# Where the row maxima, the reciprocals and the output weights' splits stand in the order of one cycle: attention mixed with a Fourier layer on one core

## The chip, the cores and the metric

One core of one Trainium2 chip runs the whole program. The metric is the device time of one execution in microseconds (us), the median of several runs. Engine names: PE is TensorE (matmuls; PEld its weight loads), DVE is VectorE, ACT is ScalarE, POOL is GpSimd, SP is the engine whose queue issues nearly all transfers here.

## The reference

Two sublayers of the same input `x` (2048 rows of 640) are mixed by a gate for each row. One is attention with 32 heads of 20 columns, the other the real part of a Fourier transform over columns and rows, as matmuls with given matrices.

```python
def _A_ref(x, wqkv, wo):                      # H = 32, Dh = 20
    qkv = (x @ wqkv).reshape(B, S, 3, H, Dh).transpose(2, 0, 3, 1, 4)
    q, k, v = qkv[0], qkv[1], qkv[2]
    scores = jnp.einsum("bhqd,bhkd->bhqk", q, k) * (Dh ** -0.5)
    o = jnp.einsum("bhqk,bhkd->bhqd", softmax(scores, -1), v)
    return o.transpose(0, 2, 1, 3).reshape(B, S, D) @ wo

def _B_ref(x, dft_seq_re, dft_seq_im, dft_hid_re, dft_hid_im):
    a = jnp.einsum("bsd,ed->bse", x, dft_hid_re)
    b = jnp.einsum("bsd,ed->bse", x, dft_hid_im)
    return jnp.einsum("ts,bse->bte", dft_seq_re, a) - jnp.einsum("ts,bse->bte", dft_seq_im, b)

g = sigmoid((x * gate_w).sum(-1, keepdims=True))
out = g * _A_ref(x, wqkv, wo) + (1 - g) * _B_ref(x, ...)
```

## The kernel before

**Units and steps.** Attention is cut into 32 units (`NU`), each a pair of heads and half of the queries, and each unit into 32 steps of two matmuls, one for each head. Every unit is walked twice. In the *maximum* walk ("m") PE computes a score tile of 128 queries by 512 keys (line 197), and DVE takes the maximum of each row (line 199, tile `mx`). In the *exp* walk ("e") PE computes the scores again, transposed and with the maxima subtracted (line 951), and ACT takes the exponential (line 953). The m walk runs `LEAD` = 41 steps ahead of the e walk.

**From maxima to the exp walk.** When a unit's last maximum is written, `s_end` notes the unit in the list `ends`. `max_nm` reduces the 64 partial maxima of each row to 16 negated ones (DVE, line 215, tile `nm`). `max_chain` transposes them on PE into a PSUM bank (line 233), DVE splits the result in two parts (lines 115 and 116, tiles `m1`, `m2`), and SP writes these as rows into the query tile `qst` (lines 241 and 242), two steps later in the order.

**Values.** `av_step` multiplies exponentials with values: four matmuls, one for each pair of head and query block (line 558), added up in one PSUM bank. `unit_end` then copies the bank out (`o`, line 565) and sets up the normalisation by steps counted from there: the row sums are stored to DRAM (`store_l`) and loaded back in another layout (`load_l`, tile `lc`), inverted on DVE (`recip`, line 579), stored and loaded spread out (`store_r`, `load_r`, tile `rb`), multiplied in on POOL (`norm`, line 589) and stored (`store_o`).

**The Fourier side** is the filler, written as a generator whose pieces PE does between the scores: first the column transform (line 380), then the row transform in seven products of eight units (`dft_step`, line 637), then the output projection (line 744). In the row transform each group of eight fills, `s`, needs a weight tile: two raw loads (`raw`, `raw2`), combined on POOL (line 517), cast on ACT and split on POOL (`part`, lines 113 and 116). In the last product `dft_step` also loads five rows of the output weights (`in_wo`, line 645) into a `raw` tile and splits them on POOL; `r` counts the fills since that load. There are three `raw` tiles.

**What sets the order.** Nothing is scheduled by cost: each engine executes in the order in which the Python code emits. The loop over cycles reads a string of `ORDERS`: "e" and "m" are one matmul of a walk, "F" a share of filler, "B" the burst. There are three stages: cycles of four steps while the column transform fills, 112 cycles of six steps (`k == 1`) while the row transform fills, and cycles of four steps for the output. In the middle stage the string has twelve "m":

```python
    ("ememeFFFFmeFFemFeFmFemFeFeFmeFFmeFFFFmmemmB", (0, 0, 0, 1, 0, 1), (1, 1, 0, 1, 0, 0)),
```

`burst` runs pending read-outs and casts, then two `av_step`s (three in the middle stage). A unit of 32 steps against cycles of six gives three cases that repeat every 16 cycles: its last maximum is the fourth, the eighth or the twelfth of a cycle, seven times each. `at_step(i, fn)` keeps a function for the moment when the e walk begins step i. `bank()` hands out the score and transpose tiles from five PSUM banks in rotation; a sixth holds the values.

Of the kernel before, what the change touches and what calls it, by code (L numbers as in the profile page):

```python
# [24 lines left out]
ND = D // P  # L25
# [5 lines left out]
NU = 2 * NP  # L31
# [46 lines left out]
def mix_kernel(ctx: ExitStack, tc: tile.TileContext, xa, wqk, wb, cdft, wo, out):  # L78
# [56 lines left out]
    def raw_tile():  # L135
        return work.tile([P, 1024], F32, name="raw", bufs=3)
# [40 lines left out]
        p, u = VISITS[n]  # L177
        return third["q"] if p == 14 else qst[place(p)][:, u * (S // 2) : (u + 1) * (S // 2)]

    mx, nms, ends, early = {}, {}, [], []  # L180
    now, later = [-1], {}

    def at_step(i, fn):
        later.setdefault(i, []).append(fn)
# [16 lines left out]
    def s_end(i):  # L201
        n, s = divmod(i, 32)
        if n < NU and s == 31:
            if now[0] < 0:
                max_nm(n)
            else:
                if early:
                    max_nm(n)
                ends.append(n)
        if s == 1 and 0 < n <= NU and now[0] < 0:  # L210
            max_chain(n - 1)

    def max_nm(n):
        nms[n] = small.tile([P, 16], F32, name="nm", bufs=2)
        dve.tensor_reduce(nms[n], mx.pop(n).rearrange("p h q c -> p (h q) c"), axis=AX.X, op=ALU.max, negate=True)
# [9 lines left out]
    def new_y(z):  # L225
        yp[z] = ps_y.tile([P, 512], F32, name=f"yp{z}")
        return yp[z]


    def max_chain(n):  # L230
        q = q_unit(n)
        pt = bank()[:16, :P]
        pe.transpose(pt, nms.pop(n), ident)  # L233
        m1 = small.tile([16, P], R, name="m1")
        m2 = small.tile([16, P], R, name="m2")
        split(m1, m2, pt, dve, dve)

        def rows():
            for h in range(2):
                b = 64 * h + KROWS  # L240
                sp.dma_start(f32(q[b : b + 1, :]), f32(m1[8 * h : 8 * h + 8, :]))
                sp.dma_start(f32(q[b + 1 : b + 2, :]), f32(m2[8 * h : 8 * h + 8, :]))

        if now[0] < 0:
            rows()
        else:
            at_step(now[0] + 2, rows)
# [196 lines left out]
    order = [1, ND + 1, 2, ND + 2, 3, ND + 3, 4, ND + 4]  # L444
# [16 lines left out]
    for n, c in enumerate(order):  # L461
        for t in range(4):
            m = 4 * n + t
# [23 lines left out]
    def a_tile(n, s):  # L487
        at[n, s] = group(n, s // HT)[:, s % HT]
        return at[n, s]
# [72 lines left out]
    def unit_end(i, n):  # L562
        p, u = VISITS[n]
        o = pa.tile([P, 512], F32, name="o", bufs=2)
        act.activation(o, av["tile"], AF.Copy)
        if n == NU - 1:
            tail["o"] = o
            return
        rb = pa.tile([P, 512], F32, name="rb")
        lc = pa.tile([P, 16], F32, name="lc")  # L570

        def store_l():
            sp.dma_start(l_scr[n], o.rearrange("(j r) c -> j r c", j=4)[:, DH])

        def load_l():
            sp.dma_start(lc, l_scr[n].rearrange("j (a b) -> (j a) b", b=16))

        def recip():
            dve.reciprocal(lc, lc)

        def store_r():
            sp.dma_start(r_scr[n].rearrange("j (a b) -> (j a) b", b=16), lc)

        def load_r():
            for j in range(4):
                sp.dma_start(rb[32 * j : 32 * j + 32, :], r_scr[n, j : j + 1].to_broadcast([32, 512]))

        def norm():
            pool.tensor_tensor(o, o, rb, op=ALU.mult)

        def store_o():
            for qc in range(2):
                for h in range(2):
                    j = 2 * qc + h
                    t0 = u * (S // 2) + qc * 512
                    r = (2 * p + h) * DH
                    sp.dma_start(o_scr[r : r + DH, t0 : t0 + 512], o[32 * j : 32 * j + DH, :])

        steps = (6, 10, 16, 23, 27, 34, 45) if n < NU - 4 else (1, 4, 7, 8, 11, 14, 16)
        for k, fn in zip(steps, (store_l, load_l, recip, store_r, load_r, norm, store_o)):  # L600
            at_step(i + k, fn)

# [11 lines left out]
    def dft_step(g):  # L614
        n, t, s = g // NS // HT, g // NS % HT, g % NS
        if s == 0:
            new_y(0), new_y(1)
            outs[n, t] = []
        if s % 8 == 0 and g // 8 + 3 < 2 * UNITS:
            cfin.append(load_c(g // 8 + 3))  # L620
        if s % 8 == 2 and g // 8 + 2 < 2 * UNITS:
            cfin[0][0]()
        if s == 8:
            for _, th, hf in PRODUCTS[n][2]:
                tt = th * HT + t
                y = None
                if (tt, hf) in signs:
                    y = apool[0].tile([P, HE], F32, name="yt", bufs=4)
                    sp.dma_start(y, y_scr[tt, :, hf * HE : (hf + 1) * HE])
                outs[n, t].append(y)  # L630
        c = cparts[g // 8]
        cs = slice((s % 8) * P, (s % 8 + 1) * P)
        a = at[n % 2, s]
        for z, (cz, az) in enumerate(((0, 0), (0, 1), (1, 0))):
            for h in range(2):
                r = slice(64 * h, 64 * h + 64)
                pe.matmul(yp[h][:, :HE], c[r, cz, cs], a[r, az], start=s == 0 and z == 0, stop=s == NS - 1 and z == 2)  # L637
            if z < 2:
                yield
        w = g % (HT * NS) - 16  # L640
        if n + 1 == len(PRODUCTS) and w >= 0:
            d, r = divmod(w, 16)
            if r == 0 and d < ND:
                wos[d] = raw_tile()[:, :D]
                sp.dma_start(wos[d], wo[:, d])
            if r == 5 and d < ND:
                raw = wos.pop(d)
                for h in range(2):
                    wos[d, h] = a_tile(1, 2 * d + h)
                    split(wos[d, h][:, 0], wos[d, h][:, 1], raw[:, h * HE : (h + 1) * HE], pool, pool)  # L650
        if s == NS - 1:
            m = apool[1].tile([P, HE], F32, name="m", bufs=2)
            y0, y1 = yp[0][:, :HE], yp[1][:, :HE]

            def read():
                act.activation(m, y0, AF.Copy)
                dve.tensor_tensor(m, y1, m, op=ALU.add)

            extras.append((now[0], read))
            for out_, y in zip(PRODUCTS[n][2], outs.pop((n, t))):  # L660
                extras.append((now[0] + 3, functools.partial(finish_y, out_, t, m, y)))
        yield
# [196 lines left out]
    for k, tt in enumerate(ROWS):  # L859
        i = out_start + 8 * k  # L860
# [72 lines left out]
    def score(kind):  # L933
        x = heads[kind]
        heads[kind] += 1
        i, z = divmod(x, 2)
        h = z ^ first[kind][(i - (LEAD if kind == "m" else 0) - 1 - base) % len(first[kind])]
        if kind == "m":
            s_mm(i, h)()
            if z:  # L940
                s_end(i)
            return
        if z == 0 and i <= total:
            begin(i)
        if i < total:
            n, s = divmod(i, 32)
            kt, qc = divmod(s, 2)
            q, k = q_unit(n), k_stack(n)
            b = 64 * h
            pt = bank()  # L950
            pe.matmul(pt, k[b : b + KROWS + 2, kt * P : (kt + 1) * P],  # L951
                      q[b : b + KROWS + 2, qc * 512 : (qc + 1) * 512], start=True, stop=True)
            act.activation(pts[n, kt, qc][:, h], pt, AF.Exp, scale=float(DH) ** -0.5)  # L953
            if z:
                end(i)

    def burst(c):
        for n in ends:
            if n not in nms:
                max_nm(n)  # L960
        k, _, i = phase(c)
        steps = 6 if k == 1 else 4
        run_extras(steps - 2)
        if k == 1:
            run_casts()
        for kt in range(i // 2, (i + steps) // 2):
            if k == 1 and ends and kt == (i + steps) // 2 - 1:
                max_chain(ends.pop(0))
            av_step(now[0], kt // NS, kt % NS, kt % NS == 0 and kt > i // 2)
        while ends:  # L970
            max_chain(ends.pop(0))
        if c in (HID - NS - 1, HID - 1):
            next_pool()
# [4 lines left out]
    for c in range(len(goals)):  # L978
        k, base, i = phase(c)
        order, *heads_ = ORDERS[k]  # L980
        first = dict(zip("em", heads_))
        early[:] = [c] if k == 1 else []
        for x, kind in enumerate(order):
            if kind == "F":
                fill(c)
            elif kind == "B":
                burst(c)
            else:
                score(kind)
            if k == 1 and x == len(order) // 2:  # L990
                run_loads(c - HID)
# [114 lines left out]
```

## Time and profile before

| what | value |
| --- | --- |
| median of 3 runs | 1869.56 us (1869.52 to 1870.79) |
| the profiled execution's own time | 1869.01 us |
| its span, first to last instruction | 1867.2 us |
| PE busy | 1850.2 us, 99% of the span |
| DVE, ACT, POOL busy | 1380.7, 1355.6, 1003.8 us |
| mean granted PE clock | 0.999 |

The span is 1.8 us under the execution's own time. A busy share is a mean over all stages. The chain that ended last follows the program back from its last instruction to what released each step, and shows where an engine other than PE set the time. A row of a timeline gives the start in us, the length in us, engine, line, operation, output and inputs, and in square brackets how long the engine had stood idle before it and what ended that. Matmuls are pipelined, so their rows overlap.

### The profile page before, as it was taken

How to read it: one execution, taken by the hardware profiler on the slowest of the kernel's cores; microseconds unless marked ns; L12 is line 12 of the kernel's file. 1: busy time of each engine (PE TensorE's matmuls, PEld its weight loads, DVE VectorE, ACT ScalarE, POOL GpSimd, SP SyncE). 2: the span in 40 equal slices, each digit the busy share in tenths (PEclk: the TensorE clock that was granted, in tenths of full speed). 3: DMA queues.
4: the chain of work that ended last, by engine and by line, in shares of the span. 5: the costliest groups of instructions: out<-in, count | busy, mean ns of one | idle time of the engine just before them, and what ended most of it. 6: DMA issues, size and time to landing. Idle time of an engine off the chain costs nothing.

```text
span 1867.2 us, 44796 instructions
## 1 busy us (share of the span) xinstructions
PE 1850.2 (99%) x17606; PEld 1360.0 (73%) x17606; DVE 1380.7 (74%) x2309; ACT 1355.6 (73%) x2645; POOL 1003.8 (54%) x832
## 2 busy tenths in 40 slices
PE   9999999999999999999999999999999999999998
PEld 8988777677676777777777777777777777776666
DVE  3044458787887888888888888888888888888853
ACT  4222158787877888888788888788888877878885
POOL 4334532121146676344678688655668766745544
PEclk9999999999999999999999999999999999999999
DMA  7754341222134673536577586646475856532233
GB/s 234 166 142 155 135 127 54 82 61 72 50 112 126 219 220 120 156 117 193 188 198 238 151 258 193 180 137 183 129 231 187 244 173 183 187 91 54 82 98 109
DMA packets 178771, 281.61 MB, mean 151 GB/s; under 512 B 44811, under 2 KB 113547, under 8 KB 178559
## 3 DMA queue, kind: packets, MB, share of 16 engines
q1 hardware_dynamic: 177599, 276.77, 49.1%
q0 software_dynamic: 960, 1.97, 0.6%
q8 instruction: 138, 2.26, 0.5%
q14 instruction: 74, 0.61, 0.1%
HBM read 214.61 MB, written 63.52 MB: 149 GB/s over the span
## 4 chain that ended last, share of the span: by engine, by line
PE 93%; DMA 4%; DVE 1%; POOL 1%; SPq 0%; issue 0%; ACT 0%; POOLq 0%; ACTq 0%; DVEq 0%
PE ps L558 23%; PE yp L637 18%; PE ps L951 16%; PE ps L197 13%; PE yp L380 7%; PE ps L119 4%; PE ps L121 4%; PE ps L120 4%; PE yp L744 3%; DVE mx L199 1%; DMA kst<-qk_scr 1%; DMA lc<-l_scr 1%; DMA raw<-in_wo 1%; DMA raw<-in_cdft 0%; POOL part L116 0%; PE ps L233 0%
## 5 line engine op out<-in xcount | busy, mean ns | idle before, releaser
L199 DVE TENSOR_REDUCE mx<-ps 128x1 f32<-128x512 f32 x2048 | 1281.3, 684 | 318.6 <-PE ps L197 248.0
L953 ACT ACTIVATE p<-ps 128x512 f32<-128x512 f32 x2048 | 1054.3, 613 | 292.6 <-PE ps L197 167.4
L951 PE MATMUL ps<-qst,kst 62*128 62x512 f32 x1920 | 725.9, 406 | 0.1
L197 PE MATMUL ps<-kst,qst 60*128 60x512 f32 x1920 | 668.3, 411 | 1.6 <-DVE mx L199 1.6
L637 PE MATMUL yp<-x,part 64*128 64x320 f32 x5376 | 631.1, 306 | 0.0
L637 PEld LDWEIGHTS yp<-x,part 64*128 64x128 f32 x5376 | 603.5, 185 | 7.1 <-ACT raw L390 0.4
L558 PE MATMUL ps<-p,v 128*21 128x512 f32 (+1 forms) x4096 | 483.3, 596 | 0.0
L116 POOL TENSOR_TENSOR part<-raw,part 128x1024 fp32r<-128x1024 f32 (+1 forms) x128 | 287.3, 2244 | 331.2 <-ACT part L113 307.5
L951 PEld LDWEIGHTS ps<-qst,kst 62*128 62x128 f32 x1920 | 341.3, 185 | 156.4 <-DVE mx L199 86.4
L197 PEld LDWEIGHTS ps<-kst,qst 60*128 60x128 f32 x1920 | 320.0, 184 | 15.0 <-issue 4.2
L558 PEld LDWEIGHTS ps<-p,v 128*21 128x21 f32 (+1 forms) x4096 | 101.7, 100 | 236.5 <-issue 226.8
L380 PE MATMUL yp<-wb,x 64*128 64x320 f32 x1920 | 223.8, 307 | 0.0
L380 PEld LDWEIGHTS yp<-wb,x 64*128 64x128 f32 x1920 | 209.5, 186 | 6.3 <-ACT raw L390 0.3
L391 POOL TENSOR_TENSOR raw<-raw 128x320 f32<-128x320 f32 x64 | 55.6, 868 | 267.6 <-ACT raw L390 227.8
L517 POOL TENSOR_TENSOR raw<-raw,raw 128x1024 f32<-128x1024 f32 x77 | 187.5, 2435 | 0.4 <-DMA raw<-in_cdft 0.4
L113 ACT ACTIVATE part<-raw 128x1024 fp32r<-128x1024 f32 (+2 forms) x121 | 123.4, 1020 | 6.5 <-POOL raw L517 4.3
L744 PE MATMUL yp<-x,part 64*128 64x320 f32 x768 | 102.2, 308 | 0.0
L116 POOL TENSOR_TENSOR x<-araw,x 128x320 fp32r<-128x320 f32 x112 | 97.5, 877 | 1.3
L340 ACT ACTIVATE p<-ps 128x512 f32<-128x512 f32 x40 | 23.7, 597 | 101.1 <-PE ps L121 98.1
L744 PEld LDWEIGHTS yp<-x,part 64*128 64x128 f32 x768 | 91.8, 186 | 1.0
L119 PE MATMUL ps<-x,part 128*128 128x512 f32 x200 | 79.9, 400 | 2.8 <-ACT x L113 2.6
L120 PE MATMUL ps<-x,part 128*128 128x512 f32 x200 | 78.3, 392 | 0.2 <-DVE x L116 0.2
(101 smaller groups left out, 1355.8 us busy)
## 6 DMA issues: line engine op xcount, KB each, us to landing
raw<-in_cdft SPq DMA_DIRECT2D x192, 512.0 KB
araw<-a_scr SPq DMA_DIRECT2D x192, 160.0 KB
qk_scr<-p SPq DMA_DIRECT2D x40, 512.0 KB
kst<-qk_scr SPq DMA_DIRECT2D x84, 160.0 KB
qst<-qk_scr SPq DMA_DIRECT2D x84, 160.0 KB
yt<-y_scr SPq DMA_DIRECT2D x80, 160.0 KB
a_scr<-raw SPq DMA_DIRECT2D x64, 160.0 KB
y_scr<-yt SPq DMA_DIRECT2D x64, 160.0 KB
```

The lines of the kernel that those rows point to most:

```text
L116: e2.tensor_tensor(dst2, src, f32(dst1), op=ALU.subtract)
L119: pe.matmul(ps, st1, mv1, start=first, stop=False)
L120: pe.matmul(ps, st1, mv2, start=False, stop=False)
L197: pe.matmul(ps, q[b : b + KROWS, qt * P : (qt + 1) * P], k[b : b + KROWS, kc * 512 : (kc + 1) * 512], start=True, stop=True)
L199: return lambda: dve.tensor_reduce(mx[n][:, h, qt, kc : kc + 1], ps, axis=AX.X, op=ALU.max)
L380: pe.matmul(yp[h][:, :HE], x[r, xz, d, cs], w[r, wz, d, :HE], start=d == 0 and z == 0, stop=d == ND - 1 and z == 2)
L517: pool.tensor_tensor(raws[0], raws[0], raws[1], op=ALU.add if PRODUCTS[n][0][1][0] > 0 else ALU.subtract)
L558: pe.matmul(t[32 * j : 32 * j + m, :], v[:, r : r + m], pp[qc][:, h, :], start=kt == 0, stop=kt == NS - 1)
L637: pe.matmul(yp[h][:, :HE], c[r, cz, cs], a[r, az], start=s == 0 and z == 0, stop=s == NS - 1 and z == 2)
L744: pe.matmul(yp[h][:, :HE], o[oz][r], wos[d, hf][r, wz], start=d == 0 and z == 0, stop=end)
L951: pe.matmul(pt, k[b : b + KROWS + 2, kt * P : (kt + 1) * P], q[b : b + KROWS + 2, qc * 512 : (qc + 1) * 512], start=True, stop=True)
L953: act.activation(pts[n, kt, qc][:, h], pt, AF.Exp, scale=float(DH) ** -0.5)
```

## The change

Four places are edited. In the middle stage `nm` is no longer reduced directly behind a unit's last maximum: it is reduced ahead of the cycle's ninth maximum, if the unit has ended by then, and in the burst if it ends with the cycle (twelfth maximum). Only in the first case does the transpose stand ahead of the burst's last `av_step`; in the other it now comes behind it. In `unit_end` the reciprocal, its store and load and the normalisation move by 4, 2, 2 and 3 steps, for all but the last four units. The output weights are split at the eleventh fill behind their load instead of the fifth.

```diff
-    mx, nms, ends, early = {}, {}, [], []
+    mx, nms, ends = {}, {}, []
...
             else:
-                if early:
-                    max_nm(n)
                 ends.append(n)
...
-        steps = (6, 10, 16, 23, 27, 34, 45) if n < NU - 4 else (1, 4, 7, 8, 11, 14, 16)
+        steps = (6, 10, 20, 25, 29, 37, 45) if n < NU - 4 else (1, 4, 7, 8, 11, 14, 16)
         for k, fn in zip(steps, (store_l, load_l, recip, store_r, load_r, norm, store_o)):
...
-            if r == 5 and d < ND:
+            if r == 11 and d < ND:
                 raw = wos.pop(d)
...
     def burst(c):
+        ready = any(n in nms for n in ends)
         for n in ends:
             if n not in nms:
                 max_nm(n)
...
-            if k == 1 and ends and kt == (i + steps) // 2 - 1:
+            if ready and kt == (i + steps) // 2 - 1:
                 max_chain(ends.pop(0))
             av_step(now[0], kt // NS, kt % NS, kt % NS == 0 and kt > i // 2)
...
-        early[:] = [c] if k == 1 else []
...
             else:
+                if k == 1 and kind == "m" and order[:x].count("m") == 8:
+                    for n in ends:
+                        max_nm(n)
                 score(kind)
```

In the changed kernel the lines from `s_end` to the burst have numbers lower by two, and those behind the last edit higher by one.

PE's order at the burst of the first unit that ends with a cycle's twelfth maximum (`ps_9539` is that score, `ps_9560` the transpose), before:

```order
L197 MATMUL ps_9539<-kst_86,qst_88 128x512
L558 MATMUL ps_9059<-p,v 21x512 x8
L233 MATMUL ps_9560<-ident,nm 16x128
L558 MATMUL ps_9059<-p,v 21x512 x4
L951 MATMUL ps_9571<-qst_88,kst_86 128x512
L197 MATMUL ps_9575<-kst_87,qst_89 128x512
L951 MATMUL ps_9578<-qst_88,kst_86 128x512
L197 MATMUL ps_9581<-kst_87,qst_89 128x512
L951 MATMUL ps_9589<-qst_88,kst_86 128x512
```

The same place in the changed kernel:

```order
L197 MATMUL ps_9538<-kst_86,qst_88 128x512
L556 MATMUL ps_9058<-p,v 21x512 x12
L231 MATMUL ps_9563<-ident,nm 16x128
L949 MATMUL ps_9570<-qst_88,kst_86 128x512
L197 MATMUL ps_9574<-kst_87,qst_89 128x512
L949 MATMUL ps_9577<-qst_88,kst_86 128x512
L197 MATMUL ps_9580<-kst_87,qst_89 128x512
L949 MATMUL ps_9589<-qst_88,kst_86 128x512
```

The transpose has moved behind the last four `av_step` matmuls, directly ahead of the next cycle's scores; five tiles later its bank is used again, by the third exp score.

DVE's order around the same burst, with the reciprocal of an earlier unit, before:

```order
L579 RECIPROCAL lc<-lc 128x16
L199 TENSOR_REDUCE mx<-ps_9474 128x1
L199 TENSOR_REDUCE mx<-ps_9498 128x1
L199 TENSOR_REDUCE mx<-ps_9508 128x1
L199 TENSOR_REDUCE mx<-ps_9527 128x1
L199 TENSOR_REDUCE mx<-ps_9530 128x1
L199 TENSOR_REDUCE mx<-ps_9536 128x1
L199 TENSOR_REDUCE mx<-ps_9539 128x1
L215 TENSOR_REDUCE nm<-mx 128x16
L115 CAST m_9562<-ps_9560 16x128
L116 TENSOR_TENSOR m_9563<-ps_9560,m_9562 16x128
L199 TENSOR_REDUCE mx<-ps_9575 128x1
```

and in the changed kernel:

```order
L199 TENSOR_REDUCE mx<-ps_9535 128x1
L199 TENSOR_REDUCE mx<-ps_9538 128x1
L213 TENSOR_REDUCE nm<-mx 128x16
L115 CAST m_9565<-ps_9563 16x128
L116 TENSOR_TENSOR m_9566<-ps_9563,m_9565 16x128
L199 TENSOR_REDUCE mx<-ps_9574 128x1
L199 TENSOR_REDUCE mx<-ps_9580 128x1
L577 RECIPROCAL lc<-lc 128x16
L199 TENSOR_REDUCE mx<-ps_9606 128x1
```

On DVE the order around `nm` is as it was; the reciprocal has moved from behind the fifth maximum of a cycle to behind the second of the next.

POOL's order around the third of the five output weight splits (`x_24245` and `x_24362` are the tile written, the rows with two `raw` the combining additions), before:

```order
L517 TENSOR_TENSOR raw<-raw,raw_24644 128x1024
L115 CAST x_24245<-raw 128x320
L116 TENSOR_TENSOR x_24245<-raw,x_24245 128x320
L115 CAST x_24245<-raw 128x320
L116 TENSOR_TENSOR x_24245<-raw,x_24245 128x320
L771 TENSOR_TENSOR yt<-yt,m 128x320
L116 TENSOR_TENSOR part<-raw,part 128x1024
L517 TENSOR_TENSOR raw<-raw,raw_24811 128x1024
```

and in the changed kernel:

```order
L515 TENSOR_TENSOR raw<-raw,raw_24640 128x1024
L769 TENSOR_TENSOR yt<-yt,m 128x320
L116 TENSOR_TENSOR part<-raw,part 128x1024
L515 TENSOR_TENSOR raw<-raw,raw_24811 128x1024
L115 CAST x_24362<-raw 128x320
L116 TENSOR_TENSOR x_24362<-raw,x_24362 128x320
L115 CAST x_24362<-raw 128x320
L116 TENSOR_TENSOR x_24362<-raw,x_24362 128x320
L116 TENSOR_TENSOR part<-raw,part 128x1024
```

The split has moved behind the next combining addition, one weight tile later.

## The prediction

> **What bounds the kernel now.** I read the page first (its parts 1, 4 and 5), then the chain that ended last in order of time, then the timelines of DVE, PE, POOL and ACT at the places the chain points to.
>
> ```profile
> PE 1850.2 (99%) x17606; PEld 1360.0 (73%) x17606; DVE 1380.7 (74%) x2309; ACT 1355.6 (73%) x2645; POOL 1003.8 (54%) x832
> PE 93%; DMA 4%; DVE 1%; POOL 1%; SPq 0%; issue 0%; ACT 0%; POOLq 0%; ACTq 0%; DVEq 0%
> L951 PEld LDWEIGHTS ps<-qst,kst 62*128 62x128 f32 x1920 | 341.3, 185 | 156.4 <-DVE mx L199 86.4
> ```
>
> PE is busy for 1850.2 of 1867.2 us and carries 93% of the chain, so the end moves only where PE's work is held up. The change alters no arithmetic; it can win only the few per cent of the chain on DMA, DVE and POOL. The last row says that a weight load of the exp scores (L951) is itself what waits when a PSUM bank is still being read by DVE.
>
> The kernel repeats a cycle that ends in a burst of `av_step` matmuls (L558). In the chain the bursts are therefore a clock, and the distance of two starts is a cycle's length. Picked rows:
>
> ```profile
> 332.32 1.85 PE ps L558 x16
> 338.48 1.85 PE ps L558 x16
> 344.86 1.85 PE ps L558 x16
> ...
> 674.09 2.70 PE ps L558 x24
> 683.07 2.50 DVE mx L199 x4
> 693.74 2.70 PE ps L558 x24
> ...
> 721.67 2.71 PE ps L558 x24
> 731.08 2.70 PE ps L558 x24
> 740.62 1.84 PE ps L558 x16
> ...
> 778.26 2.70 PE ps L558 x24
> ...
> 1042.62 1.84 PE ps L558 x16
> ...
> 1070.53 7.42 DMA lc<-l_scr
> 1080.90 2.70 PE ps L558 x24
> ...
> 1147.39 2.70 PE ps L558 x24
> ...
> 1175.08 8.44 DMA lc<-l_scr
> 1186.54 2.70 PE ps L558 x24
> ...
> 1403.68 2.70 PE ps L558 x24
> ...
> 1451.24 2.70 PE ps L558 x24
> ...
> 1554.71 2.70 PE ps L558 x24
> ...
> 1593.86 2.50 DVE mx L199 x4
> 1604.51 2.70 PE ps L558 x24
> ```
>
> An undisturbed cycle of six steps: 693.74 to 721.67 is three cycles, 9.31 us each. A pattern of three units takes 16 cycles, about 151 us, and comes seven times in the product stage. What lies above 9.31 is what the change can reach.
>
> **The change part by part.**
>
> *1. Transpose behind the burst (seven units).* Where a unit's last maximum is the twelfth of its cycle, DVE still owes four maxima when the burst begins: the chain leaves PE for "DVE mx L199 x4" at 683.07, and so seven times, the last at 1593.86. From 674.09 to 693.74 are 19.65 us: one cycle with a reciprocal (9.41, below) and one with this transpose, 10.24, that is 0.93 over 9.31.
>
> ```profile
> 685.86 0.28 PE L233 MATMUL ps<-ident,nm 128*16 128x128 f32 x1 [0.53 <-DVE nm L215]
> ...
> 340.27 0.28 PE L233 MATMUL ps<-ident,nm 128*16 128x128 f32 x1
> 340.47 0.50 PE L951 MATMUL ps<-qst,kst 62*128 62x512 f32 x1
> 340.90 0.28 DVE L116 TENSOR_TENSOR m<-ps,m 16x128 fp32r<-16x128 f32 x1
> ...
> 667.42 0.50 PE L951 MATMUL ps<-qst,kst 62*128 62x512 f32 x1
> 668.00 0.98 PE L637 MATMUL yp<-x,part 64*128 64x320 f32 x9
> ```
>
> Of the 0.93, PE stands 0.53 at the transpose (685.86). The third `av_step` (a third of 2.70, 0.90) now runs in that gap and more than fills it. The transpose itself stays on the path. Behind a burst it stands already in the first stage: the cycle from 338.48 takes 6.38, the one before 6.16, so 0.22. One thing is new. The banks rotate by five, so the transpose's bank is wanted again by the fifth tile, the third exp score of the next cycle. In the first stage filler stands ahead of that score; here the order begins "ememe" and the score comes at once: five scores take 0.58 (667.42 to 668.00), the first begins 0.20 behind the transpose (340.27 to 340.47), so the third exp score would begin 0.78 after it. DVE has read the bank only at 341.18, 0.91 after. PE then waits 0.13, or 0.13 plus a load of 185 ns = 0.32. I take 0.25, nearer the upper, since the loads are seen waiting themselves. New excess 0.47, gain 0.46, times seven: 3.2 us. Ends: 5.0 without a bank wait (0.93 - 0.22), 1.6 with twice the price (0.93 - 0.22 - 0.48 = 0.23).
>
> The Trainium skill says (TensorE: Matmul & The Clock Gate, the section on the array's architectural detail) that PE's queue can pull weight loads ahead of running matmuls. By that rule the wait would be 0.13 alone and the sum 0.8 us better; the row of L951's loads, idle 156.4 us and mostly until DVE was done, speaks against it at a bank that is not free.
>
> Behind the transpose DVE's two small operations come later against the burst, but the maxima that they hold up are late too. The four row DMAs wait on them in SP's queue, about 0.3 later; their unit starts some ten steps on, so no cost.
>
> *2. Negated maximum ahead of the ninth maximum (seven units).* Where the unit ends with the fourth maximum, `nm` stands in a dense run.
>
> ```profile
> 736.36 0.69 DVE L199 TENSOR_REDUCE mx<-ps 128x1 f32<-128x512 f32 x1 [0.17 <-PE ps L197]
> 737.08 0.22 DVE L215 TENSOR_REDUCE nm<-mx 128x16 f32<-128x64 f32 x1
> 740.20 2.49 DVE L199 TENSOR_REDUCE mx<-ps 128x1 f32<-128x512 f32 x4 [0.42 <-PE ps L197]
> ```
>
> The run behind it is 0.2 late, banks come free late, and the cycle takes 9.54 (731.08 to 740.62): 0.23. Its new place is the pause of 0.42 ahead of the ninth maximum (740.20), longer than its 0.22. Gain 0.23 x 7 = 1.6; ends 1.0 and 1.7. Where the unit ends with the eighth maximum nothing moves.
>
> *3. Reciprocals four steps on (21 in the product stage).*
>
> ```profile
> 680.58 0.24 DVE L579 RECIPROCAL lc<-lc 128x16 f32<-128x16 f32 x1
> 680.74 1.93 DVE L199 TENSOR_REDUCE mx<-ps 128x1 f32<-128x512 f32 x3
> ```
>
> A reciprocal pushes the next maximum by 0.16 and costs a cycle 0.10 (721.67 to 731.08 is 9.41). Its new place is behind the second maximum of a cycle, where a pause of 0.17 follows one maximum later (736.36). It just fits: 0.09 x 21 = 1.9 gained; ends 0 (as dear there) and 2.1. Two of them wait for their transfer. 1042.62 to 1080.90 is 38.28, the same four cycles from 740.62 to 778.26 are 37.64: 0.64 more, with the load of `lc` landing 7.42 after its issue. 1147.39 to 1186.54 is 39.15 for four cycles, 693.74 to 731.08 is 37.34: 1.81 more, landing after 8.44. Four steps are two thirds of 9.31, 6.2 us, more than three times either wait, so 2.4 us go; ends 0.6 and 2.5.
>
> The Trainium skill puts a transfer at about 2.0 us plus its bytes over 436 GB/s (DMA: Bandwidth & Descriptors, Anatomy of one DMA), 2.02 us for these 8 KB as an estimate. By that no reciprocal would wait and this term would be nothing; here the rows measure 7.42 and 8.44.
>
> What follows a reciprocal moves too. Its store goes from step 23 to 25, five steps behind instead of seven; SP already stands waiting for the reciprocal in some units, and behind that store it stands at the row DMAs anyway, so nothing is held up. The four `rb` loads keep four steps to the store. The normalisation moves three steps on POOL and is the second rival's subject. Seven reciprocals of the first stage land in the same slot of the next cycle, at no cost.
>
> *4. Output weight splits six fills on (five, last product).*
>
> ```profile
> 1578.96 0.45 POOL L115 CAST x<-raw 128x320 fp32r<-128x320 f32 x1 [7.61 <-DMA raw<-in_wo]
> ...
> 1587.26 1.06 ACT L113 ACTIVATE part<-raw 128x1024 fp32r<-128x1024 f32 x1 [3.60 <-POOL raw L517]
> ```
>
> POOL waits 7.61 for a weight row; the combining addition behind it (L517) is late; ACT's cast waits 3.60 for that, and the exponentials queue behind the cast. 1554.71 to 1604.51 is 49.80; the same five cycles from 1403.68 to 1451.24 are 47.56. The difference is 2.24. Six fills of eight are three quarters of a cycle, about 7 us; the load itself no longer waits for a late POOL, so the wait is nearly gone: 2.2; ends 0 and 2.3. A split then holds its raw tile longer, until about five fills before the next weight load wants one: covered.
>
> **Sum.** 3.2 + 1.6 + 1.9 + 2.4 + 2.2 = 11.3 us. The profiled execution took 1869.01, so 1857.7; the runs' median is 1869.56, 0.55 above it, and the prediction is for that: 1858.3. All good ends give 13.6 (1856.0).
>
> **The rivals.** *Given back on DVE and in the banks.* The transpose wins only 1.6 and the reciprocals nothing. For it: both new places have a margin of hundredths. Then 1.6 + 1.6 + 2.4 + 2.2 = 7.8, 1861.8.
>
> *Slower: POOL falls behind.* The normalisation now comes ahead of a combining addition instead of behind one.
>
> ```profile
> 654.02 1.28 POOL L589 TENSOR_TENSOR o<-o,rb 128x512 f32<-128x512 f32 x1
> 660.44 2.43 POOL L517 TENSOR_TENSOR raw<-raw,raw 128x1024 f32<-128x1024 f32 x1
> 665.09 1.05 ACT L113 ACTIVATE part<-raw 128x1024 fp32r<-128x1024 f32 x1
> ```
>
> The addition ends at 662.87, ACT's cast begins at 665.09: 2.22 of slack, 0.94 after the 1.28 of the normalisation. Where POOL runs more than that behind, the exponentials wait. The price is near 2.0 per 3.60 of ACT's wait (part 4); to pass the 11.3 and another 3.7 it must strike with full force in eight of 21 units, 16.0 us, which ends at 1874.3. POOL is busy 54%, so unlikely.
>
> *Transfers stay late.* The waits of parts 3 and 4 meet another waiter: 3.2 + 1.6 + 1.9 = 6.7, 1862.9. Against it: both transfers landed well inside the time that is added.
>
> *No transfer ever bound.* The late reciprocals cost nothing by themselves, and PE was late for another reason at both places; without those 2.4 us, 1860.7. This is what follows if transfers take the skill's 2.02 us (the page on DMA above); the chain contradicts it twice.
>
> That the change does nothing is excluded: the orders of PE, DVE and POOL differ at just these places.
>
> **How the numbers follow.** The forecast 0.65 (its own range 1856.0 to 1861.0); given back 0.12; late transfers 0.10; no transfer bound 0.04; slower through POOL 0.04; smaller gains than any of these, within 0.2%, 0.05. A difference under 0.2%, 3.7 us, can't be told from none. Faster 0.65 + 0.12 + 0.10 + 0.04 = 0.91, same 0.05, slower 0.04. The range goes from 1 us under the good ends, 1855.0, past the late transfers with half a microsecond, 1863.5.
>
> **What the next profile would show.** Right: the seven chains through "DVE mx L199 x4" gone; PE's idle time at L233 near 0; cycles with that transpose about 9.8; none of 9.4 or 9.54; no `lc` load and no `in_wo` in the chain; ACT's wait for L517 gone. Wrong: exp scores (L951) idle at DVE's L116 behind a burst by more than 0.5; cycles still at 9.4 with the reciprocal early in them; longer waits of ACT's cast for L517; POOL waiting long for `in_wo` still.

## The result, and the profile after

The changed kernel takes 1856.76 us, median of four runs (1855.66 to 1858.53), against 1869.54 for the kernel before on the same chip (1868.96 to 1870.79): ratio 0.9932, 95% interval 0.9914 to 0.9949. Forecast were 1858.3 and a range of 1855.0 to 1863.5. The profiled execution of the changed kernel, the longest of the four, took 1858.53.

From the page of the changed kernel, PE's busy time, the chain's shares by engine, and the weight loads of the exp scores:

```profile
PE 1847.3 (99%) x17606; PEld 1362.8 (73%) x17606; DVE 1380.5 (74%) x2309; ACT 1356.0 (73%) x2645; POOL 1002.9 (54%) x832
PE 99%; DMA 0%; DVE 0%; ACT 0%; POOL 0%; SPq 0%; POOLq 0%; issue 0%; ACTq 0%
L949 PEld LDWEIGHTS ps<-qst,kst 62*128 62x128 f32 x1920 | 341.6, 185 | 154.3 <-DVE mx L199 86.4
```

The same work is on every engine, but PE now carries 99% of the chain instead of 93%. The shares of DMA, DVE and POOL, which were all that the change could reach, are gone.

The chain after, bursts (start, length, engine, line), the stretches that were shown of before:

```profile
684.20 2.70 PE ps L556 x24
693.99 2.71 PE ps L556 x24
...
731.21 2.70 PE ps L556 x24
750.17 2.70 PE ps L556 x24
...
1068.82 2.70 PE ps L556 x24
1078.11 2.70 PE ps L556 x24
...
1171.95 2.70 PE ps L556 x24
1181.23 2.71 PE ps L556 x24
...
1547.04 2.70 PE ps L556 x24
1594.33 2.70 PE ps L556 x24
```

The cycle with the late transpose is 9.79 (684.20 to 693.99; it was 10.24). 731.21 to 750.17 is 18.96 for the cycle in which `nm` stood early and the one behind it; it was 9.54 + 9.62. The two cycles whose reciprocal waited for `lc` are 9.29 and 9.28. The five cycles with the output weights are 47.29, before 49.80. From here on a cycle has a number, counted from the program's first value burst, the distance of two such starts taken from the full list of instructions; the product stage is cycles 56 to 166, and was 11.3 us shorter.

Timelines of DVE and PEld around that late transpose, and of DVE where a unit ends with the fourth maximum:

```profile
686.32 0.22 DVE L213 TENSOR_REDUCE nm<-mx 128x16 f32<-128x64 f32 x1
687.46 0.28 DVE L116 TENSOR_TENSOR m<-ps,m 16x128 fp32r<-16x128 f32 x1
687.79 0.18 PEld L949 LDWEIGHTS ps<-qst,kst 62*128 62x128 f32 x1 [0.45 <-DVE m L116]
688.87 0.23 DVE L577 RECIPROCAL lc<-lc 128x16 f32<-128x16 f32 x1
689.97 0.69 DVE L199 TENSOR_REDUCE mx<-ps 128x1 f32<-128x512 f32 x1 [0.17 <-PE ps L197]
...
739.70 0.21 DVE L213 TENSOR_REDUCE nm<-mx 128x16 f32<-128x64 f32 x1
740.09 2.48 DVE L199 TENSOR_REDUCE mx<-ps 128x1 f32<-128x512 f32 x4 [0.18 <-PE ps L197]
```

In the third row the load of the third exp score stands idle for 0.45 until DVE has read the transpose's bank at 687.74: this is the bank wait that the forecast added to the price of the move. The reciprocal and the other `nm` fit in their pauses, with 0.17 and 0.18 to spare.

### The profile page after: what moved, and what is told of

It reads as the page before. It is cut to its first block, busy times and chain, and to the rows that moved or that the text cites. A ratio compares the mean times of both kernels' runs of the same rounds, so it can differ in the third digit from the quotient of the medians.

```text
span 1856.7 us, 44810 instructions
## 1 busy us (share of the span) xinstructions
PE 1847.3 (99%) x17606; PEld 1362.8 (73%) x17606; DVE 1380.5 (74%) x2309; ACT 1356.0 (73%) x2645; POOL 1002.9 (54%) x832
## 4 chain that ended last, share of the span: by engine, by line
PE 99%; DMA 0%; DVE 0%; ACT 0%; POOL 0%; SPq 0%; POOLq 0%; issue 0%; ACTq 0%
PE ps L556 25%; PE yp L635 19%; PE ps L949 17%; PE ps L197 15%; PE yp L378 7%; PE ps L119 4%; PE ps L120 4%; PE ps L121 4%; PE yp L742 3%; DMA p<-in_xa 0%; PE ps L231 0%; DVE mx L199 0%; PE ps L1041 0%; POOL x L1010 0%; PE yp L1062 0%; POOLq L1103 0%
## 5 line engine op out<-in xcount | busy, mean ns | idle before, releaser
L951 ACT ACTIVATE p<-ps 128x512 f32<-128x512 f32 x2048 | 1054.9, 613 | 284.8 <-PE ps L197 177.2
```

## The experiments

**Four parts, one at a time.** The theory: the terms are independent, and each is worth what the sum says. The rivals give the gain of one part to another. Each ran once: 1865.44 us with the transpose alone, 1868.42 with `nm`, 1862.99 with the steps, 1867.27 with the weight splits, 1870.75 for the kernel before beside them. Transfers that are late in one execution and not in the next are in these times, so the parts are read from cycle lengths.

*The transpose alone.*

```diff
+        ready = any(n in nms for n in ends)
...
-            if k == 1 and ends and kt == (i + steps) // 2 - 1:
+            if ready and kt == (i + steps) // 2 - 1:
...
-        early[:] = [c] if k == 1 else []
+                early[:] = [c] if k == 1 and order[:x].count("m") < 11 else []
```

> The kernel before with the first edit alone: the transpose of a unit that ends with a cycle's twelfth maximum stands behind the burst; nm stays directly behind the last maximum, reciprocals and weight splits stay. My theory: the seven cycles with that transpose go from 10.24 to 9.78 us, every other cycle keeps its length (9.54 where nm follows the fourth maximum, 9.40 with a reciprocal), and the product stage is 7 x 0.46 = 3.2 us shorter. Rival: the 9.78 of the changed kernel holds a reciprocal that now falls in the same cycle and costs it 0.09 there; then these cycles take 9.69 here, 3.9 us in all. Second rival: the gain needs the moved nm or reciprocal; then they stay above 10.0.

```profile
685.25 2.70 PE ps L558 x24
695.05 2.70 PE ps L558 x24
```

9.80 here; over the seven 9.78 to 9.81, together 3.1 us. The reciprocal that the changed kernel has in the same cycle is therefore free.

*`nm` alone.*

```diff
-                if early:
-                    max_nm(n)
...
+                if k == 1 and kind == "m" and order[:x].count("m") == 8:
+                    for n in ends:
+                        max_nm(n)
                 score(kind)
```

> The kernel before with the second edit alone: nm is reduced ahead of the cycle's ninth maximum, the transpose always stands ahead of the burst's last av_step. My theory: the seven cycles whose unit ends with the fourth maximum go from 9.54 to 9.31 us, 7 x 0.23 = 1.6 us, the cycles with the late transpose stay 10.24, all others as before. Rival (the pause of 0.42 doesn't take it in, and the reciprocals' move made the room in the changed kernel): they keep 9.40 or more, at most 1.0 us in all.

```profile
730.90 2.70 PE ps L556 x24
749.84 2.70 PE ps L556 x24
...
1068.97 8.40 DMA lc<-l_scr
```

18.94 for the two cycles; the seven went from 9.54 to 9.30, 1.7 us. The last row is the load of `lc` that ends at 1077.37, in the cycle that waited 0.6 in the trace of before: here 0.9. The whole product stage was only 0.5 us shorter: the wait of cycle 116 was gone (1.8), but another, for the output weights in cycle 159, took 2.4 more than in the trace of before, and three others 0.8 more together.

*The steps alone.*

```diff
-        steps = (6, 10, 16, 23, 27, 34, 45) if n < NU - 4 else ...
+        steps = (6, 10, 20, 25, 29, 37, 45) if n < NU - 4 else ...
```

> The kernel before with the seven steps of the normalisation alone moved. My theory: the cycles with a reciprocal go from 9.40 to 9.31 us, the two that waited for lc from 9.98 and 11.24 to 9.3, cycle 159 (its reciprocal 8.5 us behind the burst's start) from 11.37 to about 11.3 since the output weights hold it; in the first stage cycle 55 goes from 9.44 to 8.45 and cycle 49 from 6.53 to 6.28, since the filler's store no longer stands on SP behind the four rb loads. Product stage 21 x 0.09 + 2.4 = 4.3 us shorter, first stage 1.2. Rival for 159: its wait is the third late lc transfer, not the weights; then it goes to 9.3 here. Rival for the first stage: the gain there is the neighbourhood of another edit or noise; then 55 stays at 9.44.

Every cycle that held a reciprocal is now 9.28 to 9.34, but for cycle 159, and no `lc` load stands in the chain. Cycle 159 is 11.77: with no reciprocal left in it, it still waits. So 159 belongs to the weights.

*The weight splits alone.*

```diff
-            if r == 5 and d < ND:
+            if r == 11 and d < ND:
```

> The kernel before with the output weights split at the eleventh fill alone. My theory: cycle 159 goes from 11.37 to 9.40 us (it keeps its reciprocal), cycle 157 stays 9.57, since 157 is 9.57 in the changed kernel too; 1.97 us in all. By the prediction's term both go, 2.24 us. Rival: cycle 159 waits for lc and not for the weights; then it stays near 11.37.

```profile
1554.86 2.70 PE ps L558 x24
1602.70 2.70 PE ps L558 x24
```

47.84 for the five cycles that took 49.80: 1.96 less, all in cycle 159 (9.42, reciprocal included). 157 stays 9.55. The term of 2.24 was too large, as it counted 157's 0.26 to the weights.

**What the steps do in the first stage.** In the changed kernel cycle 55, in which ACT does the column transform's last read-out, is 8.45 instead of 9.44, which no term of the sum had. Two single moves tell apart which step does it.

*The four `rb` loads alone: `(6, 10, 16, 23, 29, 34, 45)`.*

> The kernel before with the four rb loads alone two steps later (step 29 instead of 27). My theory: this alone takes the first stage's gain, since in the last cycle of the column transform SP then reaches the filler's store to a_scr ahead of the rb loads and ACT no longer waits 1.44 us for it: cycle 55 from 9.44 to about 8.45. The product stage keeps its reciprocals (9.40) and whatever late lc loads this execution has. Rival: the reciprocal's or the normalisation's move did it; then cycle 55 stays near 9.4.

ACT's timeline, first of before, then of this kernel:

```profile
601.32 0.77 ACT L390 ACTIVATE raw<-yp 128x320 f32<-128x320 f32 x2 [1.44 <-DMA a_scr<-raw]
```

```profile
601.94 0.78 ACT L390 ACTIVATE raw<-yp 128x320 f32<-128x320 f32 x2
```

Before, ACT waits 1.44 until a store has emptied a `raw` tile; with the loads two steps later it doesn't wait, and cycle 55 is 8.45. SP's timeline, before and then with the loads later, shows why:

```profile
591.85 1.78 SPq L586 DMA_DIRECT2D rb<-r_scr  x4
593.74 0.36 SPq L893 DMA_DIRECT2D a_scr<-raw  x1
594.14 2.07 SPq L512 DMA_DIRECT2D raw<-in_cdft  x2
596.31 0.38 SPq L893 DMA_DIRECT2D a_scr<-raw  x1
```

```profile
594.03 0.38 SPq L893 DMA_DIRECT2D a_scr<-raw  x1
594.52 1.77 SPq L586 DMA_DIRECT2D rb<-r_scr  x4
596.33 0.90 SPq L512 DMA_DIRECT2D raw<-in_cdft  x2
597.52 0.33 SPq L893 DMA_DIRECT2D a_scr<-raw  x1
```

Cycle 55 starts at 599.03 in the first trace and at 601.21 in the second. Before, the filler's first store stands behind the four `rb` loads, which wait for nothing here but take SP 1.78 to issue, and it goes out 5.3 ahead of the cycle instead of 7.2. The second of the two weight loads behind it then stands 1.2 on SP until that store has landed, and the second store, the one that ACT waits for, goes out 2.7 ahead instead of 3.7. The cause is shown: SP's order.

*The reciprocal alone: `(6, 10, 20, 23, 27, 34, 45)`.*

> The kernel before with the reciprocal alone four steps later (its store, the rb loads and the normalisation stay). My theory: all of the product stage's gain of the steps is here: cycles of 9.40 go to 9.30, and no cycle waits for lc (105, 116 and 137 at 9.30); cycle 55 stays near 9.4. Rival (the store now stands on SP three steps behind the reciprocal, so that SP blocks on it and the loads behind come late): some of those cycles, or ones behind them, exceed 9.31 by more than 0.1.

```profile
1549.31 5.62 DMA raw<-in_wo
1558.58 2.17 POOL part L116
1560.75 2.48 DMA y_scr<-yt
1564.50 2.31 POOL part L116
1566.80 12.52 DMA raw<-in_cdft
```

The reciprocal's gain is as expected (9.28 to 9.31, and 105, 116 and 137 free of `lc`), and 55 stays 9.26. Yet the run is no faster, 1871.56 against 1870.75 for the kernel before beside it: cycle 159 took 16.19. The chain shows how far: POOL, late through a weight row, gives up its `raw` tile late, the next tile's load starts at that moment and takes 12.52, and POOL's timeline has it idle for 10.96 at the next weight row (7.61 before). That this edit caused the longer chain isn't shown. The rival, SP blocked at the store behind the reciprocal, has no such wait among SP's between 1545 and 1592; and the wait for the weights differs between the other executions too, as the table has it.

Seven executions, cycle lengths in us, from the bursts' starts ("old" means at its old place):

```
execution     recip old  weights old   105    116    137    157    159
before           yes     yes           9.98  11.24   9.39   9.57  11.37
transpose alone  yes     yes           9.52   9.40   9.56   9.59  11.21
nm alone         yes     yes          10.34   9.40   9.55   9.82  13.76
rb loads alone   yes     yes           9.40   9.41   9.82   9.77  11.49
weights alone    yes     no            9.50   9.39   9.81   9.55   9.42
steps alone      no      yes           9.30   9.30   9.30   9.55  11.77
changed kernel   no      no            9.28   9.29   9.31   9.57   9.32
```

Above 9.40, the late `lc` loads cost 2.4 in the trace of before and 0.3 (0.12 + 0.16), 1.1, 0.4 and 0.5 in the four others. The weights, at the old place, cost 1.8 to 4.4 in cycle 159 (over 9.31 where the reciprocal has moved), and 6.9 with the reciprocal alone.

**How far POOL may fall behind.** The slower rival needed the normalisation to delay a combining addition by more than 0.94 us. Behind each normalisation of the changed kernel, one or two more multiplications of its size, their result unused:

```diff
             pool.tensor_tensor(o, o, rb, op=ALU.mult)
+            if n < NU - 4:
+                pool.tensor_tensor(rb, o, rb, op=ALU.mult)     # twice in the second kernel
```

> The changed kernel with a second multiplication of the same size (1.28 us) on POOL behind each normalisation, its result unused. It measures the margin that the slower rival needs. In the changed kernel the combining addition behind a normalisation ends 0.96 us ahead of ACT's cast in 14 of the 20 cycles with both, and 1.8 to 2.5 us in the others. If that is the whole margin, these 14 exceed it by 0.32 and cost 0.32 x 2.0 / 3.6 = 0.18 each, 2.5 us. If ACT and the banks have a margin of their own behind the cast, nothing is lost: every cycle within 0.05 of the changed kernel's. If the rival's price is too low (the exponentials wait in full), 0.32 each, 4.5 us.

> As the last, with two such multiplications (2.56 us) behind each normalisation. Whole margin 0.96: 14 cycles exceed it by 1.60 and six by 0.1 to 0.8, 14 x 1.60 x 0.56 = 12.5 us and about 1.5 more. In full: 14 x 1.6 = 22 us. With a margin of its own behind the cast: less than half of the 12.5.

With one, no cycle of the product stage changes by more than 0.06. With two, these change: 62, 94, 110 and 142 by 0.1 each, 68, 100, 116 and 148 by 0.83 each, 3.7 us in all. From the chain and the waits of the second:

```profile
722.18 2.38 POOL raw L515
```

```profile
ACT part L113 <- POOL raw L515: 15.3, 11, 1.6
```

That is 3.7 where the forecast's price made 12.5 to 14. The expectations' count of 14 tight cycles was wrong: the trace of the changed kernel has eight normalisations with 0.95 to 1.01 us of slack; six fall into products that need no addition, and six have 1.8 to 2.5 us. Per cycle the forecast's price holds in four of them (1.60 over the margin at 2.0 / 3.6 is 0.89, measured 0.83); the other four lose hardly anything, which no row explains, and 0.32 over the margin costs nothing at all. So this rival was further off than its own margin said.

**The bank behind the late transpose.** Two edits of the changed kernel: every transpose of the middle stage behind the burst; and that together with filler ahead of the third exp score, in the cycle behind such a transpose.

```diff
-            if ready and kt == (i + steps) // 2 - 1:
+            if False and kt == (i + steps) // 2 - 1:
...
+        if late:                  # the cycle follows a burst with a transpose behind it
+            order = order.replace("emeFFFFm", "emFFeFFm", 1)
```

> The changed kernel with every transpose of the middle stage behind the burst and the order string as it is. My theory (a late transpose costs 0.47 wherever the unit ends): the 14 cycles of 9.65 go to 9.78, 1.8 us lost, the seven stay 9.78. Rival (where nm was ready ahead of the burst, the transpose needs not wait for it and DVE reads the bank sooner): they go to 9.53 to 9.6, up to 1.7 us won.

> The changed kernel with two further edits: every transpose of the middle stage stands behind the burst (21 units, not seven), and in the cycle behind one the order begins ememFFeFF in place of ememeFFFF, so that two pieces of filler stand ahead of the third exp score, which wants the transpose's bank. My theory of the 0.47 that was left (0.22 the transpose, 0.25 the third exp score's wait for the bank): the seven cycles of 9.78 go to 9.53, and the 14 of 9.65 go to 9.53 too; 7 x 0.25 + 14 x 0.12 = 3.4 us. Rival (the 0.47 is the transpose itself and what it waits for, no bank): the seven stay 9.78 and the 14 rise to 9.78, 1.8 us lost. Second rival (the third exp score, two pieces later, starves ACT): cycles behind a burst grow by 0.1 or more.

Waits of PE's weight loads in the product stage: the changed kernel, then every transpose late (in us in total, times, longest):

```profile
PEld ps L949 <- DVE m L116: 14.2, 20, 0.8
```

```profile
PEld ps L949 <- DVE m L116: 9.6, 21, 0.5
```

Late alone: the 14 go from 9.65 to 9.80, 2.1 us lost, and all 21 wait 0.46 at that score. With the filler the row is gone from the list, the load of the third exp score doesn't wait, and all 21 cycles take 9.49 to 9.53:

```profile
685.81 0.18 PEld L949 LDWEIGHTS ps<-qst,kst 62*128 62x128 f32 x1
```

```profile
682.22 2.70 PE ps L556 x24
691.74 2.70 PE ps L556 x24
...
738.23 2.71 PE ps L556 x24
747.75 2.70 PE ps L556 x24
```

The product stage is 3.7 us shorter than the changed kernel's. Of the 0.48 that a late transpose left (mean of the seven), 0.27 was the bank and 0.21 the transpose.

The first of the two wait rows needs care: 13 of its 20 waits are not the seven late ones. They are of 0.85 each ((14.2 - 7 x 0.45) / 13), and they stand at the first load behind a burst, where the kernel before has one too in a cycle of 9.30:

```profile
667.42 0.18 PEld L951 LDWEIGHTS ps<-qst,kst 62*128 62x128 f32 x1 [0.85 <-DVE mx L199]
```

In the trace of before, 189 of the 191 waits of this line are such ones, of 0.84 or 0.85 directly behind the burst's last loads, whatever releaser the row names. So they show no bank that isn't free. Of the 0.34 that a transpose inside a burst costs (9.65 against 9.31), 0.21 is what a transpose costs behind one; the other 0.13 stay open.

That version and the changed kernel, timed beside each other:

> The kernel with every transpose behind the burst and filler ahead of the third exp score, timed. My theory: its product stage is 3.7 us shorter than the changed kernel's in the traces, so it lies that much under the changed kernel's median of 1856.76, at about 1853.1, 0.991 of the kernel before. Rival (the shorter stage meets more late transfers elsewhere): 1856 or above.

> The changed kernel again, timed beside the last on the same chip, to have both against the same runs of the kernel before. My theory: 0.993 of the kernel before, 3 to 4 us over the last. Rival (the differences in the first stages from run to run are larger than the edits): the two don't differ by more than their spread.

1854.66 us, median of nine runs, and 1857.39, median of six, with 1869.82 for the kernel before in the same call; ratios 0.9921 (0.9897 to 0.9945) and 0.9929 (0.9910 to 0.9947). The intervals overlap, so these ratios alone don't tell the two apart. One of the nine runs took 1873.74 at a granted clock of 0.949; the other eight lie between 1852.69 and 1855.50, all six of the changed kernel between 1855.71 and 1861.13. By the medians the version is 2.7 us faster than the changed kernel, and the traces' 3.7 in the product stage point the same way.

## Why the prediction was right

```
term of the sum             forecast   traces before/after   alone
transpose behind burst        3.2        7 x 0.45 = 3.2       3.1
nm ahead of ninth maximum     1.6        7 x 0.25 = 1.7       1.7
reciprocals early             1.9        21 x 0.10 = 2.1      1.9 (in 20 of the 21)
reciprocals that wait         2.4        0.58 + 1.84 = 2.4    0.3 to 1.1 in other executions
output weights                2.2        1.97                 1.96; 1.8 to 6.9 in other executions
sum                          11.3       11.3 (product stage)
cycle 55, SP's order          0          0.99                 0.99
```

**The clock of bursts was the right view.** Each gain was read as a difference of two cycle lengths, and none needed a busy time; only the late transpose's new price was added up from rows.

**The bank wait was sized right, but not by the row that was called on for it.** 0.25 was taken between 0.13 and 0.32, and 0.27 measured; that it came so near is in part luck. The row of L951's loads, idle 156.4 us, was read as waits for banks that DVE still reads, and decided for the upper end. Nearly all of its waits are the 0.85 behind the bursts, which undisturbed cycles have as well, so the row said nothing on this. What bears the choice out is the trace after: the load of the third exp score is the one that waits, 0.45, until DVE has read the bank. The Trainium skill's rule that PE's queue can pull weight loads ahead of running matmuls (TensorE: Matmul & The Clock Gate, architectural detail) would, by the prediction's estimate from it, have made the cycle 9.66; it is 9.78.

**"No transfer ever bound" fell.** `lc` loads stand in the chains of four executions with the early reciprocal: 7.42 and 8.44 us before, 8.40 with `nm` alone, 8.19 and 8.15 with the weights and with the `rb` loads alone. The Trainium skill's rule (DMA: Bandwidth & Descriptors, Anatomy of one DMA), which that section fits to transfers issued by GpSimd, gives an estimate of 2.02 us; these loads are issued by SP, beside this kernel's other traffic, and took about four times that.

**"Given back", "Transfers stay late" and "POOL falls behind" fell** by the rows of the result (0.17 and 0.18 us of pause left; 9.28 and 9.29 in the waiting cycles) and by the two doses on POOL.

**What was off.** First, term 4: 2.24 counted the whole excess of five cycles, 0.26 of which stays in 157; the reciprocals, 2.1 for 1.9, happened to make up for most of it. Second, the two waiting reciprocals: 2.4 is right for the profiled execution alone, and it was carried over to the median undiminished. The weights were dearer in four of the other five executions with the old place than in the profiled one, which may have made up for it; the runs without a profile can't show it. That the sum held for the median too was in part luck. Third, "seven reciprocals of the first stage land in the same slot of the next cycle, at no cost" looked at DVE alone; by the trace they are six, and a seventh moves in the last stage. The step that failed is the sentence "the four `rb` loads keep four steps to the store": true, but what else stands on SP's queue beside them was not asked, and that was worth 1.0: cycle 55 is 9.08 to 9.50 in the five traces with these loads at the old place, and 8.44 to 8.45 in the nine others. What the prediction did say of SP held: SP stands longer at the store of the reciprocals (84.3 us in all, 34.9 before), and no cycle of the product stage is longer for it.

The profiled executions differ by 10.5 us, the medians by 12.8. Between the traces: 11.3 in the product stage and 1.3 in the first stage less (1.0 of it cycle 55; cycle 49 varies from 6.16 to 7.25 with no edit that explains it), but 2.2 more ahead of the first burst (258.01 and 260.24), in code that the change doesn't touch. Over all fourteen traces that part took 257.0 to 260.7, in no order that follows the edits, and the part behind the product stage 206.2 to 206.3. Without that part 11.3 + 1.0 = 12.3 are left, near what the medians show.

**Left open.** The 0.26 of cycle 157. It stays with the weights, the steps or the transpose changed; in both traces of the version with the filler 157 is 9.31, and cycle 97 is 9.55 instead. No row names what PE waits for there.

## What to carry to other kernels

Where one engine carries the chain, measure the length of a repeating cycle by one instruction in the chain, and price every edit as a difference of cycle lengths; but take a wait for a transfer from several executions, as it can be 0.3 in one and 2.4 in the next. When a step moves, read each queue that it stands in, the DMA issuing one above all: four loads took 1.78 to issue here, and the store behind them, and what waited for it, came late. When an operation moves next to a dense run of tiles, count the banks in rotation to the tile that wants its bank again, and put other work ahead of that one.

## What the hardware showed that was not expected

- The same 8 KB load on the same spot decided the time in one execution and not in the next: cycle 116 took 11.24 in one trace with the old reciprocal, and 9.39 to 9.41 in four.
- The wait for one weight row cost 1.8 us in one execution and 6.9 in another (cycle 159 at 11.21 and 16.19), POOL standing 7.21 and 10.96 for it, with a load of 12.52 us on the way in the second. That a late POOL makes its own next load late is read from the chain, not tested.
- Weight loads show an idle time of 0.85 behind nearly every burst, with DVE named as what ended it, in cycles that lose nothing: a long row of waits is not a loss until a cycle length says so.
- The code ahead of the first value burst varies by 3.7 us between executions, more than any term of the sum; the 206.2 us behind the product stage by 0.1.
